# Loading q, k and v by pairs of tiles, two tokens to a partition, in a fused attention and maxout-FFN kernel on one NeuronCore

## The chip, the cores and the metric

The kernel runs on one core of one Trainium2 chip. The metric is the device time of one execution in microseconds; the number given for a kernel is the median of its runs. A core has five engines that run queues of their own and wait for each other through semaphores: PE (TensorE: matmuls, transposes), DVE (VectorE), ACT (ScalarE), POOL (GpSimd) and SP (SyncE, which here only issues DMAs). Each engine takes its instructions strictly in the order of its queue, so an instruction that waits holds all that stand behind it on that engine.

## The reference

Sliding-window attention with a few global keys, and after it a feed-forward layer that takes the maximum of three products. Four batches, 8 heads, 768 tokens, 64 elements to a head; 3072 tokens of 512 in the FFN; all f32 in DRAM.

```python
scores = scale * np.matmul(q, k.transpose(0, 1, 3, 2))
is_global = pos[None, :] < 8                     # n_global
is_local = (rel >= 0) & (rel < 96)               # n_local; rel = query - key
dist = np.where(is_global & ~is_local, 96.0, np.abs(rel))
scores = np.where(is_global | is_local, scores - slopes[h] * dist, -1e9)
a = softmax(scores)
x = (a @ v).transpose(0, 2, 1, 3).reshape(3072, 512)
h = np.maximum(np.maximum(x @ w1, x @ w2), x @ w3)      # 512 -> 768, three times
out = h @ w_out                                         # 768 -> 512
```

## The kernel before, in words

**Tiles.** The 3072 tokens are 24 tiles T of 128 (six to a batch; t is T's place in its batch). A query tile needs the keys of its own tile and of the one before (`ds` = 0 and 1 in `u_S`, L267); the 8 global keys are put into the key columns 0 to 7 of the middle tiles (`put_kg`, L208) and the same rows of v (`put_vg`, L217), where the window would leave them out. g is a group of four heads. Tiles are gathered into seven FFN chunks of 4, 2, 2, 4, 4, 4 and 4 tiles (`sizes`, L89), so an FFN product has a free width of 512, or 256 in chunks 1 and 2.

**One tile's path.** `load` (L159) fetches q and k of a tile, `load_v` (L168) v, each row of 64 f32 (256 bytes) to its own place, one token to a partition. For the first 12 tiles `load_part` (L150) fetches q and k of groups of 2 or 4 tiles (`GROUPS`, L91), with 2 or 4 tokens to a partition, and `u_x` (L225) puts the tokens into their plain order when it copies the transposes out of PSUM (the strided copy at L242). `cast` and `cast_part` make bf16 of it. q and k come to have the head's elements on the partitions either by PE transposes (`u_x` L238, `u_X` L260) and a copy out of PSUM (L242, L262, L263, L265), or by a DMA transpose (L249, from SP's queue). Then:

- S: scores of one g into one two-bank PSUM slot (L282), 16 matmuls for the two g of a tile with t > 0; ACT's exp from PSUM into `P` (L287).
- M: `P` times a mask that has the decay, the window and the global keys in it (L306, L308, DVE). The masks are made in the head from `rbase`, the distances (L452 to L471), by ACT (`u_K`, L299). Some early tiles have a bias added by a matmul instead (`u_B` L294, L274) and skip M.
- A: `P` times v with a column of ones, 16 matmuls (8 where t is 0; L321, L324), into one of the same two slots; then the reciprocal and the product that divides (L330, L331, DVE) into `xb`.
- T: `xb` transposed, by PE (L348) and a copy (L349) or by DMA (L339), into `xT`.
- F: one of 18 units of a chunk (6 column blocks f, 3 weights j), four matmuls (L360) into one PSUM bank. j = 0 is copied to SBUF by ACT (L365), j = 1 and 2 are maxima on DVE (L367, L369), the last into `ht`.
- O: six matmuls of one output tile (L375), a copy out (L381), and the output DMA. E is the last chunk's outputs: two tiles' sums are first run over five of the six rows of `ht`, then over the last.

**PSUM.** Two two-bank slots for S and A (`sp0`, `sp1`), three banks `h` for F and O, one bank `tp` for transposes: eight banks. A pool hands out its buffers in turn, and a unit issues its PE work and the operation that empties the bank together.

**The order of the work** is written out by hand: `SCHEDULE` (L25 to L57) is a list of units, each a letter and numbers, and `tc.manual_schedule()` takes them in that order, which is the order on every engine's queue. The last number of many units names the engine: 0 ACT, 1 DVE, 2 POOL, 3 and 4 special ways (for `X` and `T` 4 is the DMA transpose). So `F3.4.1` is chunk 3, block 4, weight 1, and `C14.1.2` the cast of tile 14's v on POOL.

```python
def u_F1(c, f, j):
    ...
    for dm in range(4):
        nc.tensor.matmul(ps, w123[f // 2][:, dm, j, ...], xT[c][:, dm], ...)
    if j == 0:
        nc.scalar.copy(h01, ps)
    elif j == 1:
        nc.vector.tensor_max(h01s[c, f], h01s[c, f], ps)
    else:
        nc.vector.tensor_max(ht[c][:, f], h01s[c, f], ps)
```

Of the kernel before, what the change touches and what calls it, by code (L numbers as in the profile page):

```python
# [60 lines left out]
def kernel(  # L61
# [18 lines left out]
    assert NG == 8 and NL == 96  # L80
# [21 lines left out]
    raw_pool = ctx.enter_context(tc.tile_pool(name="raw", bufs=5))
    rawv_pool = ctx.enter_context(tc.tile_pool(name="rawv", bufs=6))
    cast_pool = ctx.enter_context(tc.tile_pool(name="cast", bufs=5))
    qkT_pool = ctx.enter_context(tc.tile_pool(name="qkT", bufs=2))
    p_pool = ctx.enter_context(tc.tile_pool(name="pp", bufs=6))
    z_pool = ctx.enter_context(tc.tile_pool(name="zz", bufs=4))
    xb_pool = ctx.enter_context(tc.tile_pool(name="xb", bufs=3))
    xT_pool = ctx.enter_context(tc.tile_pool(name="xT", bufs=3))
    stage_pool = ctx.enter_context(tc.tile_pool(name="stage", bufs=3))  # L110
    ht_pool = ctx.enter_context(tc.tile_pool(name="ht", bufs=2))
    h01_pool = ctx.enter_context(tc.tile_pool(name="h01", bufs=4))
    ost_pool = ctx.enter_context(tc.tile_pool(name="ost", bufs=6))
    psS = ctx.enter_context(tc.tile_pool(name="psS", bufs=1, space=bass.MemoryType.PSUM))
    psH = ctx.enter_context(tc.tile_pool(name="psH", bufs=3, space=bass.MemoryType.PSUM))
    psT = ctx.enter_context(tc.tile_pool(name="psT", bufs=1, space=bass.MemoryType.PSUM))
# [42 lines left out]
    def load(T):  # L159
# [5 lines left out]
        for i, src in enumerate((q, k)):  # L165
            nc.sync.dma_start(out=r[:, i], in_=src[b, :, sl, :].rearrange("h s d -> s h d"))
# [344 lines left out]
```

## Time and profile before

| | |
|---|---|
| median of 3 runs | 181.25 us (181.25 to 181.27) |
| span of the profiled execution | 179.4 us |
| time of the profiled execution | not given on the page; the median stands 1.85 us above the span |
| first and last FFN matmul (L360) start | 23.5 and 170.3 us |
| busy: PE, DVE, ACT, POOL | 169.3, 121.2, 103.1, 38.0 us |
| HBM read, written | 25.17 MB, 6.29 MB |
| loads of q, k, v by tile, 256 KB each | 48, landing 4.3 to 5.1 us after issue (medians) |
| loads of q, k by part, 512 KB each | 12, landing 7.2 to 7.5 us after issue (medians) |
| DMA transposes on SP | 9 of qkT, 11 of xT; 1.2 us each to issue |

The profile is one execution. A line of a group gives the source line, the engine, the operation and its tiles with their shapes, the count, the busy time and the mean length of one, and then the idle time of that engine just before these instructions with what ended it. "PE h L360 <- DVE h L367" in a list of waits means that PE's matmul at L360 waited for DVE's operation at L367. The chain is followed back from the last instruction: each piece is the work, or the wait, that the next one could not start without. The stretch tables give the busy time of each engine between two moments, the clock that was granted to PE (1.00 is full) and the moved bytes.

### The profile page before, as it was taken

The numbers are of one execution on the slowest core, as the hardware profiler recorded it, in microseconds if no ns is written. First come the engines' busy times: TensorE is split into PE (matmuls) and PEld (weight loads), VectorE is DVE, ScalarE is ACT, GpSimd is POOL, SyncE is SP. The second block draws the span as 40 slices with busy tenths as digits, with TensorE's granted clock in tenths as the row PEclk, the third lists the DMA queues.
The fourth block names the chain that finished last, engine by engine and source line by source line (L and its number), as shares of the span: only waits on it lengthen the run. The fifth ranks groups of instructions, "written<-read, shape, count | busy, mean of one in ns | idle before, by whom it ended". The sixth has DMA issues, their size and how long they took to land.

```text
span 179.4 us, 3954 instructions
## 1 busy us (share of the span) xinstructions
PE 169.3 (94%) x1534; PEld 97.0 (54%) x1556; DVE 121.2 (68%) x240; ACT 103.1 (57%) x158; POOL 38.0 (21%) x64
## 2 busy tenths in 40 slices
PE   7788798999999999999999999999999999999992
PEld 2365653557877687844555455455444555444451
DVE  4636948987788879748879447979358886136610
ACT  4899697336897858565745836361772643440131
POOL 6254225532512011410007024100030301000000
PEclk9969999999999999999999999999999999999999
DMA  4999999999993999999644999869859884600005
GB/s 139 290 263 250 358 322 382 318 361 345 249 189 123 254 264 218 209 177 237 111 90 117 133 242 247 173 131 182 177 130 282 169 139 146 235 28 4 0 32 202
DMA packets 83586, 35.51 MB, mean 198 GB/s; under 512 B 66160, under 2 KB 78320, under 8 KB 83568
## 3 DMA queue, kind: packets, MB, share of 16 engines
q1 hardware_dynamic: 83424, 35.20, 82.9%
q8 instruction: 12, 0.20, 0.5%
q10 hardware_dynamic: 144, 0.07, 0.1%
q14 instruction: 6, 0.05, 0.1%
HBM read 25.17 MB, written 6.29 MB: 175 GB/s over the span
## 4 chain that ended last, share of the span: by engine, by line
PE 81%; SPq 5%; DVE 5%; DMA 3%; ACT 2%; issue 2%; ACTq 0%
PE h L360 49%; PE po L375 17%; PE sp L282 5%; DMA rawp<-in_k_dram 3%; SPq L157 3%; PE op L321 3%; PE op L324 2%; SPq L173 2%; DVE P L306 2%; PE tpp L238 1%; PE xtp L348 1%; DVE xb L331 1%; ACT P L287 1%; ACT h L365 1%; DVE qkT L242 1%
## 5 line engine op out<-in xcount | busy, mean ns | idle before, releaser
L360 PE MATMUL h<-xT,w 128*128 128x512 bf16 (+1 forms) x491 | 99.9, 348 | 1.3 <-DVE h L367 0.6
L360 PEld LDWEIGHTS <-w 128*128 128x128 bf16 x504 | 46.8, 98 | 41.3 <-issue 0.9
L287 ACT ACTIVATE P<-sp 128x1024 bf16<-128x1024 f32 (+1 forms) x48 | 43.3, 955 | 18.2 <-PE sp L282 17.8
L367 DVE TENSOR_TENSOR h<-h,h 128x512 bf16<-128x512 bf16 (+1 forms) x42 | 25.4, 610 | 23.7 <-PE h L360 15.8
L365 ACT CAST h<-h 128x512 bf16<-128x512 f32 (+1 forms) x42 | 21.7, 532 | 23.0 <-PE h L360 22.4
L375 PE MATMUL po<-wo,ht 128*128 128x512 bf16 (+2 forms) x147 | 33.0, 362 | 0.5
L306 DVE TENSOR_TENSOR P<-P,wmask 128x1024 bf16<-128x1024 bf16 x37 | 25.9, 730 | 6.3 <-ACT P L287 6.2
L369 DVE TENSOR_TENSOR ht<-h,h 128x512 bf16<-128x512 bf16 (+1 forms) x42 | 25.1, 607 | 4.0 <-PE h L360 3.3
L375 PEld LDWEIGHTS <-ht 128*128 128x128 bf16 x156 | 14.1, 98 | 13.9
L381 ACT COPY ost<-po 128x512 f32<-128x512 f32 (+2 forms) x19 | 10.6, 562 | 18.0 <-PE po L375 17.9
L331 DVE TENSOR_TENSOR xb<-op,rz 128x512 bf16<-128x512 f32 x24 | 16.6, 692 | 0.8
L282 PE MATMUL sp<-qkT 64*128 64x128 bf16 x352 | 15.0, 220 | 1.6 <-ACT qkT L242 1.4
L282 PEld LDWEIGHTS <-qkT 64*128 64x128 bf16 x352 | 10.2, 95 | 10.1 <-issue 8.0
L321 PEld LDWEIGHTS <-P 128*128 128x128 bf16 x192 | 12.7, 99 | 2.5 <-DVE va L188 0.4
L197 POOL CAST qkb<-raw 128x1024 bf16<-128x1024 f32 x7 | 7.2, 1036 | 28.5 <-DMA raw<-in_k_dram 28.5
L321 PE MATMUL op<-va,P 128*128 128x65 bf16 x160 | 12.5, 193 | 0.5 <-ACT P L287 0.3
L220 POOL COPY va<-vaf 8x260 int32<-8x260 int32 x13 | 6.5, 501 | 27.8 <-PE op L324 27.8
L242 ACT COPY qkT<-tpp 128x1024 bf16<-128x1024 bf16 (+1 forms) x10 | 9.5, 971 | 3.6 <-PE tpp L238 3.4
L324 PEld LDWEIGHTS <-P 128*128 128x128 bf16 x160 | 10.4, 97 | 1.7 <-issue 0.2
L324 PE MATMUL op<-va,P 128*128 128x65 bf16 x128 | 9.9, 193 | 0.0
L381 DVE COPY ost<-po 128x512 f32<-128x512 f32 (+1 forms) x7 | 4.4, 631 | 7.4 <-PE po L375 7.4
L188 POOL CAST va<-rawv 128x512 bf16<-128x512 f32 x9 | 5.5, 616 | 15.7 <-DMA rawv<-in_v_dram 15.5
(68 smaller groups left out, 116.2 us busy)
## 6 DMA issues: line engine op xcount, KB each, us to landing
rawv<-in_v_dram SPq DMA_DIRECT2D x24, 256.0 KB, 5.1
out_dram<-ost SPq DMA_DIRECT2D x23, 256.0 KB, 2.4
rawp<-in_q_dram SPq DMA_DIRECT2D x6, 512.0 KB, 7.2
rawp<-in_k_dram SPq DMA_DIRECT2D x6, 512.0 KB, 7.5
wst<-in_moe_w_dram SPq DMA_DIRECT2D x3, 1024.0 KB, 9.9
raw<-in_q_dram SPq DMA_DIRECT2D x12, 256.0 KB, 4.3
raw<-in_k_dram SPq DMA_DIRECT2D x12, 256.0 KB, 5.0
wst<-in_moe_w_dram SPq DMA_DIRECT2D x3, 512.0 KB, 8.9
```

Of the source, the lines that this page charges most:

```text
L282: nc.tensor.matmul(sp[:, hh, j2, ds], qT(T - ds, 1)[hsl, jp], qT(T, 0)[hsl, jp], start=not how, stop=True, skip_group_check=True)
L287: nc.scalar.activation(P[:, :, 0:n], sp.rearrange("p a b d n -> p (a b) d n")[:, :, 0:n], AF.Exp, bias=0.0, scale=scale)
L306: nc.vector.tensor_mul(P, P, wmask[:, g, :, 0:2])
L321: nc.tensor.matmul(o, P[:, i, 0], heads(va[T])[:, h], start=True, stop=(t == 0), skip_group_check=True)
L324: nc.tensor.matmul(o, P[:, i, 1], heads(va[T - 1])[:, h], start=False, stop=True, skip_group_check=True)
L331: nc.vector.tensor_tensor(out=x.rearrange("p (g h) d -> p g h d", g=2), in0=o4[:, :, :, 0:64], in1=rz[:, :, :, None].to_broadcast([128, 2, ...
L360: nc.tensor.matmul(ps, w123[f // 2][:, dm, j, (f % 2) * 128:(f % 2) * 128 + 128], xT[c][:, dm], start=(dm == 0), stop=(dm == 3))
L365: nc.scalar.copy(h01, ps)
L367: nc.vector.tensor_max(h01s[c, f], h01s[c, f], ps)
L369: nc.vector.tensor_max(ht[c][:, f], h01s[c, f], ps)
L375: nc.tensor.matmul(po, ht[c][:, f, tt * 128:(tt + 1) * 128], wo[:, f, cols], start=(f == 0), stop=(f == NF - 1))
L381: copy(ost, po)
```

## The change

All 24 tiles are loaded by pairs: a load `l` fetches q, k or v of two tiles (512 KB, or 256 KB for half of the heads in the first pair's q and k), with two neighbouring tokens on a partition, so that a run in DRAM is 512 bytes. Partitions 0 to 63 then hold the first tile of the pair, 64 to 127 the second. The order of the tokens inside a tile (the even ones, then the odd ones, e = 0 and 1) is kept: in q, k, v, the masks (`rbase` is made for that order), the scores, `xb` and `xT`; the FFN's last maximum writes `ht` with a step of two and so restores the plain order. v is cast by halves (one tile and one e, 64 partitions). `put_vg` becomes two copies.

The loads, casts, transposes and their copies out of PSUM, and the operations that empty the banks of S, A, F and O, are units of their own now, and each unit names the buffer it takes (`@slot`). PSUM is a ring `h` of four banks (F, O and the transposes) and two two-bank slots `sp` (S and A). The engine of h's first copy is chosen by the unit. DMA transposes are 14 of q and k (128 columns in, 16 blocks of 64 out) and 16 of `xb`. `SCHEDULE` is new as a whole.

```diff
-    def load(T):
...
-        for i, src in enumerate((q, k)):
-            nc.sync.dma_start(out=r[:, i], in_=src[b, :, sl, :].rearrange("h s d -> s h d"))
+    def u_l(slot, a, G, p):
+        h0, nh = span(p)
+        b, g = divmod(G, NT // 2)
+        r = ring("rv" if a == 2 else "r", slot, [128, 1024], FP32, "raw" + "qkv"[a])
+        r = r[:, 0:nh * 128].rearrange("i (h x) -> i h x", h=nh)
+        raw[a, G, p] = r
+        src = (q, k, v)[a][b, h0:h0 + nh, g * 256:(g + 1) * 256, :]
+        nc.sync.dma_start(out=r, in_=src.rearrange("h (i e) d -> i h (e d)", e=2))
+    def u_c(slot, a, G, p, how):
...
+        dst = qb[G][:, a, h0 // 2:(h0 + nh) // 2].rearrange("i j e (s d) -> i j e s d", s=2)
+        copies[how](dst, raw[a, G, p].rearrange("i (j s) (e d) -> i j e s d", s=2, e=2))
+    def u_v(slot, T, e, how):
+        G, t = divmod(T, 2)
+        src = raw[2, G, 2][64 * t:64 * t + 64].rearrange("i h (e d) -> i e h d", e=2)[:, e]
+        copies[how](heads(va(T))[64 * e:64 * e + 64, :, 0:D], src)
+    def u_x(slot, G, a, p):
...
+        for j in range(nh // 2):
+            for e in range(2):
+                nc.tensor.transpose(tp[:, :, j, e], qb[G][:, a, h0 // 2 + j, e], identb)
+    def u_X(slot, T):
...
+        nc.sync.dma_start_transpose(
+            out=qkT[G][:, t].rearrange("c a j (e i) -> c (a j e) i", e=2),
+            in_=qb[G][64 * t:64 * t + 64].rearrange("i a j e x -> i (a j e x)"))
+    def u_V(slot, T, how):
+        b, t = divmod(T, NT)
+        for e in range(2):
+            rows = slice(64 * e, 64 * e + NG // 2)
+            copies[how](words(va(T)[rows]), words(va(b * NT)[rows]))
+    def u_f(slot, c, f, j, how):
...
+            copies[how](h01, ps)
         elif j == 1:
             nc.vector.tensor_max(h01s[c, f], h01s[c, f], ps)
         else:
-            nc.vector.tensor_max(ht[c][:, f], h01s[c, f], ps)
+            dst = tile_ht(c, slot)[:, f].rearrange("p (t i e) -> p t e i", e=2, i=64)
+            nc.vector.tensor_max(dst, h01s[c, f].rearrange("p (t e i) -> p t e i", e=2, i=64),
+                                 ps.rearrange("p (t e i) -> p t e i", e=2, i=64))
-        pos = [psH.tile([128, DM], FP32, name="po", tag="h") for _ in range(min(2, n - 1))]
+        def bank(w):
+            h[0] += 1
+            return ring("h", (slot + h[0] - 1) % RINGS["h"], [128, w], FP32, "po")
...
+        for ds in range(2):
+            for e, P in halves:
+                nc.gpsimd.iota(rbase[P, ds], base=128 * ds - e, pattern=cols, channel_multiplier=-2,
+                               allow_small_or_imprecise_dtypes=True)
+        for e, P in halves:
+            nc.gpsimd.affine_select(rbase[P, 0], rbase[P, 0], base=-e, ...)
+            nc.gpsimd.affine_select(rbase[P, 0], rbase[P, 0], base=NL - 1 + e, ...)
+            nc.gpsimd.affine_select(rbase[P, 1], rbase[P, 1], base=NL - 129 + e, ...)
```

Three places of the new queue, as far as the prediction speaks of them. Small letters that follow a unit's capital empty its bank (`e` S, `n` A, `t` and `u` T, `f` F, `o` O, `s` the output DMA; `x` and `y` transposes and their copy); `Z` and `X` are DMA transposes.

```diff
-    D3.0 K4 K0 l1.0 B1.2 B2.1 D5.6 B7.1 K2 l1.1 K1 B0.1 D2.0 K3 v0 K5 D0.6 B3.1 B5.1 c0.0.1 D4.0 K6 c1.0.2
...
+    l1.0.0@0 l1.0.1@1 B6.2 B5.2 c1.0.1.1@0 K7 B7.2 D6.512@0 l0.0.1@2 K0 c0.0.1.2 D6.512@1 l0.0.0@3 K2
+    c0.0.0.2 K3 l2.0.2@0 B3.1 c1.0.0.1 K1 B2.1 K4 x0.1.1@2 x0.0.1@3 l0.1.2@4 l1.1.2@5 K6 x0.1.0@0 B4.1
...
-    F4.1.2 C17.1.2 O3.1.1 A17.1 F4.2.2 F4.3.2 S18.0.0 M18.0 S18.1.0 M18.1 F4.4.0 T16.4 T17.4 F4.4.1
...
+    S18.0.0@1 S18.1.0@0 e18.1@4 s0.2 s0.1 e18.0@5 F4.2.2@0 f4.5.1.1 S17.0.0@0 e17.0@0 v20.1.2 f4.1.1.1
+    v18.1.1 S17.1.0@1 e17.1@2 l1.11.2@0 F4.2.0@2 m18.1.1 V16.2 f4.1.2.1 F4.2.1@3 f4.2.0.1@3 S19.1.0@0
...
-    F6.4.1 F6.2.2 F6.3.2 F6.5.0 F6.4.2 F6.5.1 F6.5.2 E
+    f6.0.2.1 F6.5.0@3 F6.2.2@2 f6.2.1.1 s5.1 s4.3 f6.2.2.1 f6.5.0.0@1 F6.5.1@1 f6.5.1.1 f6.5.2.1 E@4
```

More of the change, by code (lines that the diff above doesn't have):

```diff
@@ L98, with ring @@
         chunks.append(list(range(first, first + n)))
-    NCH = len(chunks)
-    persist = ctx.enter_context(tc.tile_pool(name="persist", bufs=1))
[L102 to L116, printed above, removed]
+    last = len(chunks) - 1
+    pools = {}
+    for name in RINGS:
+        space = {"space": bass.MemoryType.PSUM} if name in ("sp", "h") else {}
+        pools[name] = ctx.enter_context(tc.tile_pool(name=f"p_{name}", bufs=1, **space))
+    persist = ctx.enter_context(tc.tile_pool(name="persist", bufs=1))
+    def ring(name, slot, shape, dtype, label):
+        assert 0 <= slot < RINGS[name]
+        return pools[name].tile(shape, dtype, name=label, tag=f"{name}{slot}")
     identf = persist.tile([128, 128], FP32, name="identf")
@@ L389, in u_E, with u_O, u_o @@
[L389 to L396 removed]
+    def u_O(slot, c, tt):
+        pos[c, tt] = ring("h", slot, [128, DM], FP32, "po")
+        f2_mm(pos[c, tt], c, tt, range(NF))
+    def u_o(slot, c, tt, how):
+        osts[c, tt] = ring("ost", slot, [128, DM], FP32, "ost")
+        copies[how](osts[c, tt], pos[c, tt])
```

458 lines of the change are left out of this document (210 added, 248 removed).

## The prediction, made before the changed kernel was run

> **What bounds the kernel now.** I read the busy shares first, then the chain of work that ended last, then that chain in order of time, the busy times by stretch, and last the costs of single operations. The page of the profile:
>
> ```profile
> span 179.4 us, 3954 instructions
> PE 169.3 (94%) x1534; PEld 97.0 (54%) x1556; DVE 121.2 (68%) x240; ACT 103.1 (57%) x158; POOL 38.0 (21%) x64
> ...
> PE 81%; SPq 5%; DVE 5%; DMA 3%; ACT 2%; issue 2%; ACTq 0%
> ```
>
> PE is busy 94% and the chain is 81% PE. The pieces of the chain in order of time (start, length, what) show where it is not:
>
> ```profile
> 10.26 6.25 DMA rawp<-in_k_dram
> 27.80 2.49 DVE P L306 x2
> ...
> 155.12 7.55 PE h L360 x35
> 162.72 7.93 PE h L360 x36
> 170.66 2.81 PE po L375 x13
> 173.52 2.37 PE po L375 x22
> ```
>
> Until 16.5 us the chain is loads; from the first FFN matmul (L360, at 23.47 in the timeline) it is PE without a break but for one stall of .6 us at 30 us, to the last copy, which starts at 175.95; its output DMA ends the span 3.45 us later. So there are three parts: head 23.47, body 152.5, tail 3.45. The busy times by stretch say how near the other engines are:
>
> ```profile
> 31.00:60.00 29.00, 28.79 (x307) 19.79 (x311) 23.98 (x46) 18.88 (x31) 9.66 (x12) 1.00 0.96 265
> 60.00:100.00 40.00, 39.69 (x428) 25.05 (x436) 31.25 (x65) 25.73 (x43) 7.79 (x13) 1.00 0.95 181
> 100.00:140.00 40.00, 39.58 (x306) 19.60 (x310) 26.91 (x50) 21.14 (x31) 5.26 (x7) 1.00 0.90 191
> ```
>
> After the stretch and its length the columns are PE, weight load, DVE, ACT, POOL, clock, DMA share, GB/s. PE is full; DVE is next, 24.0 of 29 us (83%) early on, 67% later. A change that takes work from PE gains it only while DVE keeps up.
>
> The span is 179.4; the runs' median is 181.25. The page gives no time for the profiled execution, so I put 1.85 us around the span, before and after alike. Differences of 0.2% (.36 us) are about what a measurement here can tell from none.
>
> **PE: what goes.** The qk transposes fall from 120 to 80 and those of xb from 52 to 32, as ten more tiles go by DMA transposes. Nearly all is behind the first FFN matmul: 108 transposes there become 48. In the chain a group of eight took .45 us, so one is .056, and 60 are **−3.3 us**. All other matmuls keep number and shape (S 352, A 352, FFN 504, O 156, by their weight loads), but for four bias matmuls of the head, which lies behind loads anyway.
>
> **DVE: what comes.** 17 copies of h to h01 move from ACT (11 of 512 at .686 as the maximum of that shape, 6 of 256 at .417: 10.0); v casts go from 3 to 18 because each now covers 64 partitions and one of two tokens (15 x .424 = 6.4; I price a half by its elements per partition, since the 8-partition memset of rbase took .17 and the 128-partition copy .15); four more output copies (4 x .688 = 2.8); masks 44 to 46 (1.2). Off go four qk casts less two halves (−1.9), two biases (−.9), three V copies (−.8) and some G, xT, qkT and rbase copies (−2.8). Sum **+14**, 121 to 135.
>
> ```profile
> L306 DVE TENSOR_TENSOR P<-P,wmask 128x1024 bf16<-128x1024 bf16 x37 | 25.9, 730 | 6.3 <-ACT P L287 6.2 <-ACT wmask L299 0.2
> L367 DVE TENSOR_TENSOR h<-h,h 128x512 bf16<-128x512 bf16 x30 | 20.4, 686 | 20.8 <-PE h L360 13.4 <-ACT P L287 7.3
> L369 DVE TENSOR_TENSOR ht<-h,h 128x512 bf16<-128x512 bf16 x30 | 20.1, 683 | 2.8 <-PE h L360 2.1
> ...
> L381 DVE COPY ost<-po 128x512 f32<-128x512 f32 x6 | 4.1, 688 | 3.2 <-PE po L375 3.2
> ...
> L242 DVE COPY qkT<-tpp 128x1024 bf16<-128x1024 bf16 x2 | 2.4, 1219 | 0.0
> ...
> L265 DVE COPY qkT<-tp 128x1024 bf16<-128x1024 bf16 x1 | 0.7, 683 | 0.0
> ```
>
> What counts is where it falls. I summed each stage's units, in queue order, with these row prices. Chunks 1 and 2 (256 wide, six maxima for .437 us of matmuls each): DVE 31.2 before, 35.8 after; PE 33.5 after, 35.1 with the small gaps that the chain shows behind scores. Operations standing back to back start every .60 to .64 us where each is booked at .69, so the 35.8 are some 32 to 33 of work against 35.1 of PE: 93%. At 83% nothing was lost; here each late release of a bank is a PE stall. Floor 0 (DVE always finds the next bank ready), ceiling 4 (every operation at its booked length plus the .2 us from a matmul's end to its reader's start): **+1.2**, nearer to the floor, because the pitch is measured. Chunk 4: DVE 24.2 against 25.4 of PE (before 20.5 and 26.5): 0 to 1.5, **+.3**. Chunks 3, 5 and 6 stay under 83%: 0.
>
> **ACT and POOL.** ACT loses some 19 us and is bound nowhere in the body. POOL goes from 38 to about 60: 19 more V copies at .50, nine more v casts at .616, two biases at 1.42, casts of the rest. It is still at a third; the cover is its idle time, and without it a late cast delays a transpose two tiles ahead. SP issues 22 loads less and ten DMA transposes more (1.24 each); it waits for nothing but free buffers, and the next output DMA stands behind a transpose that waits for its cast: cost 0 while the six output stages have room, one landing (D) if not.
>
> **Waits in the new queue.** Scores and outputs of attention share two slots of two banks each, and the queue has S18, one FFN unit, S17. S17.0 needs the slot of S18.1, whose exp takes 1.03 (row L287) plus .2 to start: 1.23 against .86 of FFN. S17.1 needs the slot of S18.0, whose exp stands behind the first on ACT: .75 more. **+1.1**, floor .4 if ACT starts on the other exp first. Two A units (A10, A14) stand 1.15 us behind scores in their slot: **+.2**, 0 to .3.
>
> At the end, E takes bank 0 first, that of the last third product of chunk 6 (F6.5.2). Its maximum is the last of the queue on DVE, behind that of F6.5.1, PE's last unit before E. So E begins .2 + .62 + .69 + .05 = **+1.6** after F6.5.1. Before, E started at 170.49 while the last maximum ran to 171.38, since only the sixth step of its sums reads that row and its banks were free. Floor .9 (only one maximum left to wait for), ceiling 1.8. Three reuses of a bank after one FFN unit in chunk 6 have .86 for .95: **+.2**.
>
> **Head.** Loads of 512-byte runs replace v's and part of q's and k's 256-byte ones. In the first half of the trace stretches of v and weight loads moved 230 to 384 GB/s, so order, not rate, decides; the first pairs land as before. But rbase now takes four iotas (.235 each) and six selects (.295), as halves of 64 partitions at the full price: ready at 5.2, not 3.64. Behind it three biases stand on POOL (1.42 each, to 9.4) and ahead of POOL's first q casts, so S0 is at 11 where it was at 9.34; the queue then has slack on ACT, and by my walk the exps of tile 3 end at 21.5 and the first FFN matmul follows POOL's V copies and weight cast at 24.0 (23.1 if a POOL bias is the .55 of a DVE one, 25.8 with all late): **+.5**. The clock there, from the busy times by stretch:
>
> ```profile
> 11.00:13.00 2.00, 1.82 (x21) 1.56 (x18) 1.35 (x3) 2.00 (x3) 1.20 (x2) 0.50 1.23 276
> ```
>
> The granted clock was .50 here, behind a thin stretch. Another gap may put such a stretch later, at up to +.8; it is inside the 25.8. [...]
>
> **Sum.** −3.3 + 1.2 + .3 + 1.1 + .2 + 1.6 + .2 + .5 = **+1.8**: span 181.2, time **183.0**.
>
> **Rivals.**
> A. *Faster: DVE keeps up, and PE's gain stays.* If the .62 pitch holds in chunks 1 and 2 and ACT's lighter load lets S17's slots come free, the sum is −3.3 + 1.6 + .2 + .5 = −1.0, and with the old .6 stall gone and the head .4 early rather than .5 late, −2.5: 178.7 to 180.2, middle **179.5**. For it: DVE had 5 us idle in 29 where it was fullest. It decides at a DVE load of about 95% in chunks 1 and 2. Against: the same row's waits for PE do not go away.
>
> B. *The last maximum slows.* L362 of the changed kernel writes ht with a step of two elements. The two PSUM copies above cost 1219 strided and 683 not. The maximum takes 683 for 512 elements, 1.33 ns each, the slow copy's 1.19: it has no fast rate to lose, so I take 0. Doubled, 30 x .54 + 12 x .28 = 19.6 more DVE, of which half is cover: about **192**. [...]
>
> C. *POOL slows DVE's masks.* M took .68 alone (18.28), .96 beside a POOL cast (11.90), two took 2.49 at 27.80 with POOL busy throughout. POOL's 22 us more, mostly beside masks, would add .28 to .56 to a dozen of them, about 3.6 of DVE, of which the two tight stages pass on 1.5: **184.5**. [...]
>
> D. *Loads or DMA transposes late.* Each transpose took SP 1.24 to issue and landed 3.2 later; ten more, and the queue's pairs land later than single tiles. One of them in the open adds 3.2 to the forecast: **186**.
>
> **How the numbers follow.** Forecast .45, A .30, C .12, B .05, D .08. From the forecast's own spread (181.2 to 184.8) .06 falls within 0.2% and .01 below, from A .02 within: faster .29, same .08, slower .63. The range leaves out B, A's lowest, and the far ends of C and D: 178.9 to 187.0.
>
> **What would show it.** First FFN matmul at 24.0 (not before 23.1); in PE's waits about 1.6 us on the last maximum before E, some 1.1 on an exp at S17, several short ones on DVE in chunks 1 and 2; DVE busy about 135; L362 at 683; M's mean at or under .75 (over .85 is C). It would be wrong if PE has no waits for DVE in chunks 1 and 2 (A), or if the waits are for loads (D).

## The result, and the profile after

The changed kernel took 189.55 us (median of 4 runs, 188.52 to 190.77) against 181.26 (181.25 to 181.48): ratio **1.0456** [1.0413, 1.0498]. The forecast was 183.0, the range 178.9 to 187.0. Of kernels 2, 5, 8 and 10 further down one execution in four was disturbed and of 12 two; the ratios leave these out, so 12's rests on two executions.

The page of the changed kernel:

```profile
span 187.4 us, 3816 instructions
PE 169.3 (90%) x1470; PEld 95.0 (51%) x1492; DVE 138.5 (74%) x266; ACT 87.1 (46%) x131; POOL 66.0 (35%) x104
...
PEclk9955579999999999999999999999999999999999
...
PE 70%; DVE 12%; POOL 5%; DMA 5%; issue 4%; ACT 2%; SPq 1%; POOLq 0%; DVEq 0%
```

PE has the same busy time in 8 us more, and its part of the chain is 70% instead of 81%. The clock row tells where: the four slices of 4.7 us from 9 to 28 us are below 9. The matmul records show the three parts of the span:

| us | before | after |
|---|---|---|
| first FFN matmul starts (end of the head) | 23.47 | 29.68 |
| from there to PE's last matmul's start | 152.2 | 154.2 |
| from there to the end of the span | 3.8 | 3.5 |

So **6.2 us are lost in the head and 2.0 in the body**. The head's chain, in order of time (start, length, what), pieces under .9 us left out:

```profile
5.77 1.54 POOL bias L283
...
7.37 1.34 POOL bias L283
...
8.95 1.06 issue
...
10.67 1.46 PE tp L205 x12
...
17.67 1.71 PE tp L205 x16
...
23.83 0.97 PE sp L251 x2
...
28.58 1.05 POOL w L426
```

The "issue" at 8.95 is POOL's third bias (the records have the three from 5.77 to 9.95). Then come POOL's first q cast and the transposes that wait for it. What PE waited for, of the whole span (total, times, longest), shows that wait and the body's three:

```profile
PE tp L205 <- POOL qb L188: 4.2, 1, 4.2
PE po L367 <- DVE ht L362: 1.6, 1, 1.6
PE h L343 <- ACT ost L381: 1.6, 1, 1.6
PE xtp L328 <- DVE xb L313: 1.2, 2, 1.0
...
PE po L367 <- DVE xT L331: 0.9, 1, 0.9
```

The busy times by stretch (columns as in the prediction) show PE thin and the clock at half:

```profile
8.00:16.00 8.00, 3.81 (x44) 2.86 (x44) 4.58 (x12) 4.92 (x9) 5.31 (x7) 0.54 1.19 292
16.00:24.00 8.00, 6.49 (x68) 4.76 (x68) 6.40 (x12) 3.77 (x5) 3.50 (x5) 0.50 1.09 356
24.00:32.00 8.00, 7.34 (x92) 4.47 (x92) 5.80 (x11) 5.81 (x8) 6.59 (x9) 0.90 1.09 355
```

PE's 3.81 us of 8 is at .54, no engine is full, and DMA is at 1.1 to 1.2 throughout. In the kernel before, the stretch from 8 to 16 us had PE busy 6.23 and the clock at .79:

```profile
8.00:16.00 8.00, 6.23 (x81) 4.45 (x79) 3.23 (x6) 7.51 (x10) 4.51 (x6) 0.79 1.25 267
```

In the body I summed the pitch from one weight load to the next by the kind of the first (1,344 loads of before and 1,284 of after):

| us in the body | FFN (504) | outputs (155) | S (280) | A (296) | transposes |
|---|---|---|---|---|---|
| before | 93.2 | 29.5 | 9.8 | 11.8 | 7.9 (108) |
| after | 96.9 | 31.3 | 10.1 | 12.2 | 3.6 (48) |

The transposes give 4.2 us, more than the 3.3 forecast. This is spent again: 3.7 in FFN pitches and 1.8 in those of the outputs, which is where PE's waits fall.

### The profile page after: what moved, and what is told of

Its sections match the earlier page's. It is cut to its first block, busy times and chain, and to the rows that moved or that the text cites. A ratio compares the mean times of both kernels' runs of the same rounds, so it can differ in the third digit from the quotient of the medians.

```text
span 187.4 us, 3816 instructions
## 1 busy us (share of the span) xinstructions
PE 169.3 (90%) x1470; PEld 95.0 (51%) x1492; DVE 138.5 (74%) x266; ACT 87.1 (46%) x131; POOL 66.0 (35%) x104
## 4 chain that ended last, share of the span: by engine, by line
PE 70%; DVE 12%; POOL 5%; DMA 5%; issue 4%; ACT 2%; SPq 1%; POOLq 0%; DVEq 0%
PE h L343 41%; PE po L367 14%; PE sp L259 5%; PE op L301 3%; PE tp L205 3%; DMA out_dram<-ost 3%; DMA rawv<-in_v_dram 2%; DVE P L275 2%; PE op L304 2%; DVE ht L362 2%; DVE xb L313 2%; POOL bias L283 2%; ACT P L266 1%; DVE vaf L193 1%; PE sp L251 1%
## 5 line engine op out<-in xcount | busy, mean ns | idle before, releaser
L362 DVE TENSOR_TENSOR ht<-h,h 128x512 bf16<-128x512 bf16 (+1 forms) x42 | 26.8, 646 | 6.2 <-PE h L343 5.6
L357 ACT CAST h<-h 128x512 bf16<-128x512 f32 (+1 forms) x25 | 13.1, 537 | 30.0 <-PE h L343 29.0
L239 POOL COPY va<-vaf 4x260 int32<-4x260 int32 x32 | 13.8, 430 | 31.2 <-PE op L304 27.4
L259 PE MATMUL sp<-qkT 64*128 64x128 bf16 x352 | 16.5, 231 | 1.5 <-ACT P L266 0.8
L193 POOL CAST va<-rawv 64x512 bf16<-64x512 f32 x20 | 14.2, 711 | 8.5 <-DMA rawv<-in_v_dram 5.2
L188 POOL CAST qb<-rawq 128x1024 bf16<-128x1024 f32 (+1 forms) x10 | 12.3, 1237 | 4.7 <-DMA rawq<-in_q_dram 4.4
L357 DVE CAST h<-h 128x512 bf16<-128x512 f32 (+1 forms) x17 | 10.1, 592 | 4.5 <-PE h L343 4.3
L301 PE MATMUL op<-va,P 128*128 128x65 bf16 x160 | 13.2, 197 | 0.1
L188 POOL CAST qb<-rawk 128x1024 bf16<-128x1024 f32 x7 | 7.6, 1079 | 14.3 <-issue 9.4
L381 ACT COPY ost<-po 128x512 f32<-128x512 f32 x10 | 5.9, 587 | 13.9 <-PE po L367 8.3
L233 POOL COPY qkT<-kg 128x32 bf16<-128x32 bf16 x7 | 2.0, 287 | 28.3 <-PE sp L259 25.3
```

Source lines behind the costliest of these rows:

```text
L188: copies[how](dst, raw[a, G, p].rearrange("i (j s) (e d) -> i j e s d", s=2, e=2))
L193: copies[how](heads(va(T))[64 * e:64 * e + 64, :, 0:D], src)
L259: nc.tensor.matmul(sp[:, hh, j2, ds], qT(T - ds, 1)[hsl, jp], qT(T, 0)[hsl, jp], start=not how, stop=True, skip_group_check=True)
L301: nc.tensor.matmul(o, P[:, i, 0], heads(va(T))[:, h], start=True, stop=(t == 0), skip_group_check=True)
L357: copies[how](h01, ps)
L362: nc.vector.tensor_max(dst, h01s[c, f].rearrange("p (t e i) -> p t e i", e=2, i=64), ps.rearrange("p (t e i) -> p t e i", e=2, i=64))
```

## The experiments

First FFN matmul and last matmul (starts) are from each run's profile. Where two kernels have the same PE queue, I compare the starts of the n-th weight load in both; a step in that difference is a stall, or a stretch at a lower clock, that only one of them has. "A10" in an expectation is the unit A of tile 10, and so on. Each kernel has one profile. Kernels with the same head had their first FFN matmul at 29.37 to 29.89 (changed, 4, 5, 8), at 26.92 to 27.33 (6, 7, 9) and at 26.57 and 27.16 (11, 12), so a difference under some .6 us in that column says nothing.

| kernel | ratio to before [95%] | first FFN | last matmul |
|---|---|---|---|
| before | 1 | 23.47 | 175.65 |
| changed | 1.0456 [1.0413, 1.0498] | 29.68 | 183.89 |
| 1 biases behind the q casts | 1.0419 [1.0402, 1.0437] | 27.68 | 183.00 |
| 2 zeros | 1.0427 [1.0407, 1.0446] | – | – |
| 3 both | 1.0444 [1.0425, 1.0462] | 28.85 | 184.00 |
| 4 other bank for E | 1.0397 [1.0366, 1.0428] | 29.89 | 183.21 |
| 5 two early output DMAs | 1.0532 [1.046, 1.0604] | 29.37 | 186.11 |
| 6 head in another order | 1.0383 [1.0332, 1.0433] | 27.16 | 182.39 |
| 7 = 4 + 5 + 6 | 1.0227 [1.0204, 1.025] | 27.33 | 179.86 |
| 8 h's first copy on ACT | 1.0597 [1.0559, 1.0635] | 29.38 | 188.31 |
| 9 = 7 + v of pair 8 early | 1.0274 [1.0232, 1.0317] | 26.92 | 180.57 |
| 10 = 9 without biases | 1.0289 [1.0272, 1.0306] | – | – |
| 11 = 10 + zeros in the head | 1.0323 [1.0299, 1.0348] | 26.57 | 182.01 |
| 12 = 11 + copy of tile 7 on ACT | 1.0204 [1.0179, 1.0229] | 27.16 | 179.54 |
| 13 before, v first | 1.0089 [1.0074, 1.0104] | 26.39 | 177.81 |
| 14 before, POOL biases | 1.0083 [1.0057, 1.0109] | 25.97 | 177.38 |
| 15 k first | 1.0305 [1.026, 1.035] | 28.29 | 181.38 |
| 16 = 15 + zeros | 1.0267 [1.0245, 1.0288] | 27.35 | 180.66 |
| 17 before, rbase by halves | 1.0062 [1.0046, 1.0079] | 25.1 | 176.5 |
| 18 before, 13 + 14 + 17 | 1.0176 [1.0161, 1.0192] | 27.86 | 179.3 |

### The POOL biases and the clock (1, 2, 3)

```diff
-    l1.0.0@0 l1.0.1@1 B6.2 B5.2 c1.0.1.1@0 K7 B7.2 D6.512@0 ...
-    c0.0.0.2 K3 l2.0.2@0 B3.1 ...
+    l1.0.0@0 l1.0.1@1 c1.0.1.1@0 K7 D6.512@0 ...
+    c0.0.0.2 B6.2 B5.2 B7.2 K3 l2.0.2@0 B3.1 ...
```

> The changed kernel with its three POOL biases (1.34 to 1.54 us each, 5.77 to 9.95) put behind POOL's two first q casts instead of ahead of them. Theory 1 (the biases start the loss: PE idles 4.2 us to 10.67, and the clock is at .50 from 8.5 to 25.5): q casts at about 7, PE's wait shrinks to 1 or 2 us, the granted clock stays at 1.00 or comes back by 14, first FFN matmul at 24 to 26 where it was 29.7, time 184 to 186 against 189.5. Rival (the head is bound by loads, by POOL's V copies and weight cast at 26 to 29.6, or by the pairs as such): the first FFN matmul moves by less than 1.5 us, time over 188.

The second has one unit more (`D16.512@1` ahead of `x0.0.1@3`), the third both edits.

> The changed kernel with 16 matmuls of zeros (128x512) in PE's queue ahead of the transposes that wait for POOL's q cast; nothing else moved, so the cast still ends at 10.63. If the clock is most of the loss: it stays at 1.00 past 10.7, the PE work from 10.7 to 25.5 (12 us busy at .50) shrinks to 6, first FFN matmul at 25 to 27, time 185 to 187. If the wait itself is most of it, or if the clock drops anyway because PE is thinly used from 13 to 20: the first FFN matmul stays past 28.5, time over 188.3.

> Both edits: biases behind the q casts and 16 matmuls of zeros ahead of the transposes. If wait and clock add: first FFN matmul at 23.5 to 25, time 183 to 184.5. If they are one cause (the wait is what drops the clock), the same as the biases alone, within .5 us, and the zeros (3.5 us at full clock) may even cost up to 1 us where the q cast comes before they end.

The casts went to 7.3, and the first FFN matmul came 2.0 us sooner; the time fell by under .4% and neither expectation held. Theory 1 was a third of the 6.2 at most. With the zeros too the clock held to 16.5 us and was at half for 3.4 us where the changed kernel has 17.1, and still the first FFN matmul was at 28.85, later than without: the zeros delayed the transposes to 9.95. So neither edit finds the larger part. In the same profile POOL's cast of pair 2's q stands in the chain:

```profile
20.68 0.61 POOL va L193
...
21.33 0.72 POOL va L193
...
22.11 3.00 POOL qb L188
...
25.15 1.08 PE tp L205 x16
```

A cast of 128x1024 that takes 1.04 us by itself took 3.00 beside DVE's work, and it stood behind a copy (L239) that waited 5.8 us for A1. By its ratio the zeros alone (2) changed nothing measurable.

### E's bank (4)

```diff
-    ... f6.5.0.0@1 F6.5.1@1 f6.5.1.1 f6.5.2.1 E@4
+    ... f6.5.0.0@1 F6.5.1@1 f6.5.1.1 f6.5.2.1 E@6
```

> The changed kernel with E's first bank moved from 0 (that of F6.5.2, emptied by the last maximum on DVE) to 2 (F6.2.2, emptied long before). Theory (PE's wait of 1.56 us ahead of E is for the bank alone): the wait goes, since two sums over five rows of ht (2.2 us) cover the last maximum; span 1.5 us shorter, time 188.0 against 189.5. Rival (E waits for the last row of ht anyway, or the next banks make it wait later): no more than .5 us.

By the weight loads E came 1.67 us sooner relative to the last FFN matmul, and its wait is gone from PE's list. Of it .7 shows in this span: the head was .2 later here, and the waits near 100 us .8 longer. The next experiments look at that place.

### The head's order, the output stage, DVE's copies (5 to 8)

```diff
 5
-    ... e13.0@1 l1.7.2@5 ...      s0.0 v16.1.1 s1.1 F4.1.0@1 ...
+    ... e13.0@1 s0.0 s1.1 l1.7.2@5 ...      v16.1.1 F4.1.0@1 ...
 6
-    x0.0.0@1 B1.1 K5 y0.1.1.1@0 y0.1.0.1 G0.1 v1.1.2 y0.0.1.0 S0.1.0@0 ...
-    ... A0@0 ... c0.1.2.2@1 w1.1@1 m1.1.1 n0@0 t0@2 x1.0.2@3 l2.2.2@2 c1.1.2.1 x1.1.2@0
-    u0.0@0 m1.0.1 A1@1 V1.2 v3.0.2 y1.1.2.1@1 n1@1 v3.1.2 c0.2.2.2@2 ...
+    x0.0.0@1 B1.1 K5 y0.1.1.1@0 y0.1.0.1 G0.1 v1.1.2 v1.0.2 c0.1.2.2@1 B6.2 B5.2 B7.2 y0.0.1.0 S0.1.0@0
+    ... x1.0.2@3 A0@0 ... c1.1.2.1 y1.0.2.0@1 m1.1.1 n0@0 x1.1.2@0 t0@2 l2.2.2@2
+    u0.0@0 m1.0.1 y1.1.2.1 B0.1 S2.1.0@0 e2.1@4 A1@1 c0.2.2.2@2 V1.2 v3.0.2 n1@1 ...
 8 (17 times)
-    f0.4.0.1@2
+    f0.4.0.0@2
```

> The changed kernel with two output DMAs (tile 0 of chunk 0 and tile 1 of chunk 1) issued on SP at about 75 us, where their sums have been copied out, and not at about 103 behind four DMA transposes and two v loads. Theory (PE's 1.6 us at 107, matmul of chunk 4 behind ACT's output copy, is a missing output stage: the copy waits for the landing, 4.8 us, of an output DMA that SP issued late): PE's wait on the output copy goes, 1.1 to 1.7 us less, about 188.0 against 189.5. Rival (the DMA queue as such is late there, and v's or the transposes' landings stop PE next): under .5 us.

> The changed kernel with the same units in the head in another order: POOL casts q and v of the first pairs ahead of its three biases, and q of pair 2 ahead of the copy of the global rows of v that waits for A1; DVE casts v and multiplies the first masks ahead of a bias; PE transposes pair 1 ahead of T0; the scores of tile 2 come ahead of A1. Theory 2 (the head's loss is in the order: units that wait stand ahead of units that could go): first FFN matmul at 24 to 26 (29.7 in the changed kernel, 27.7 with the biases alone moved), span 2 to 4 us shorter, time 186 to 187.5, as part of it is lost again at the late output DMA at 103. Rival (POOL's and DVE's work in the head has grown too large for any order: 19 us of POOL before the first FFN matmul): first FFN matmul at 27 or later, time over 188.3.

> The new order of the head, the two early output DMAs and the other bank for E together. If the three losses are separate (head 3.5 to 5.5, output stage 1.1 to 1.7, E 1.6): 182 to 184. If a further bound stands behind them (DVE in chunks 1 and 2, v loads): over 185.

> The changed kernel with its 17 copies of h's first product on DVE given back to ACT (as before the change): DVE 10 us less, ACT 9 us more. If DVE is what the body waits for in chunks 1, 2 and 4, as the prediction has it: .5 to 1.5 us shorter, about 188.5. If DVE's load costs nothing there: no change or up to 1 us longer, as the copies stand behind exps of 1.03 us on ACT.

**5**: the wait for the output copy went, and another of 2.2 us came 5 us ahead of it. What PE waited for from 30 us on:

```profile
PE po L367 <- DVE ht L362: 2.2, 1, 2.2
PE po L367 <- DVE xT L331: 0.9, 1, 0.9
PE sp L259 <- DVE xb L313: 0.2, 1, 0.2
```

and the chain ahead of it in the same kernel:

```profile
98.28 0.56 SPq L334
...
98.87 4.96 DMA rawv<-in_v_dram
...
103.86 0.42 DVE va L193
...
104.31 0.74 DVE ht L362
...
105.09 2.01 PE po L367 x6
```

SP issues v of pair 8 at 98.87, behind DMA transposes (L334); it lands 4.96 us later; DVE's cast of it stands in DVE's queue ahead of chunk 3's last maximum, and PE's outputs of chunk 3 wait for that. The theory (a missing stage) was true of the one wait and wrong about the time. The six matmuls at 105.09 take 2.01 where six take 1.3 at full clock (.216 each): behind this wait the granted clock was at half for 3.4 us. The clock rows of 5, 8 and 11 show such a stretch in the body, each behind a wait of 1.8 to 2.4 us (from 105.9 us in 5, 106.6 in 8, 93.3 in 11):

```profile
PEclk9955899999999999999999699999999999999999
```

```profile
PEclk9755799999999999999999699999999999999999
```

```profile
PEclk9999969999999999999969999999999999999999
```

The changed kernel, whose waits there are 1.6 us at most, has none behind 26 us.

**6**: the first FFN matmul at 27.16, the time 188.35, 1.2 us less. Theory 2 expected 24 to 26 and 186 to 187.5; these are, by a hair, the numbers of its rival (27 or later, over 188.3), that the work of POOL and DVE is too large for any order. **7** brings PE's last matmul 4.0 us sooner than in the changed kernel (179.86 for 183.89): 2.4 of it in the head, the rest in the body. Its time of 185.47 misses the 182 to 184 expected of it.

**8** fell the other way: ratio 1.0597, though DVE was busy 9 us less (129.4). By the weight loads it loses .5 at 50, .6 at 54 and .8 at 60 us, where copies now stand behind exps, and 3.1 at 103, at the load of v, about half of this by the half clock. The wait of .9 for tile 7's copy stays. So chunks 1 and 2 wait as before with less work on DVE, and the copies are better there.

### SP's queue, biases, zeros, tile 7 (9 to 12)

```diff
 9
-    ... f3.1.1.1 X14@3 ...      Z13@1 l2.8.2@2 m15.0.1 ...
+    ... f3.1.1.1 l2.8.2@2 X14@3 ...      Z13@1 m15.0.1 ...
10 (and all eight B units go)
-    S3.0.1@0 e3.0@0 S3.1.1@1 e3.1@2 v2.0.1 m2.1.1 m2.0.1 ...
+    S3.0.0@0 e3.0@0 S3.1.0@1 e3.1@2 v2.0.1 m2.1.1 m2.0.1 m3.0.1 m3.1.1 ...
11 (six more like it)
-    S0.1.0@0
+    D5.512@2 S0.1.0@0
12
-    u7.1@2
+    u7.0@2
```

> The kernel with the new order of the head, the two early output DMAs and the other bank for E, and now also v's load of pair 8 issued on SP two DMA transposes and one wait earlier (ahead of the DMA transposes of tiles 14, 15 and 16 and not behind them). Theory 3 (the body's loss at 100 us is SP's queue: the load is issued at 97 to 100 because it stands behind transposes that wait for casts; DVE then waits for v with the last maximum of chunk 3 behind it, and PE's output sums for that maximum, 1.6 to 2.2 us): PE's wait at 100 us goes, 183.5 to 184.2 against 185.5. Rival (the DMA engines are full there, so v lands no earlier): within .5 us of 185.5.

> The kernel before it in this list, with no biases at all: the scores of tile 3 are multiplied by the mask as those of the other tiles are (two more masks on DVE, .68 each), and the eight biases (three on POOL 4.4 us, five on DVE 1.9 us) and four bias matmuls go. If POOL's and DVE's load holds the head: first FFN matmul .5 to 1.5 us sooner than 27.3, time 182.5 to 183.5. If the head is a chain of waits (exp, mask, A, division, transpose) with idle engines beside it: within .4 us.

> As without biases, and 24 matmuls of zeros (128x512) in PE's gaps from 8 to 19 us, so that the granted clock holds: it was .50 from 10 to 23 us in the kernel with the new order, where PE was busy 15 of 20 us. Theory 2b (with the waits gone, the halved clock sets the rest of the head: 6 us of work at .50 that would take 3): clock 1.00 through 20 us, first FFN matmul at 24 to 25.5, time 180.5 to 182. Rival (PE's work at half speed is hidden behind ACT, DVE and POOL): under .5 us of gain, or a loss as the zeros delay transposes.

> As the kernel before it in this list, and the copy of tile 7's transposed x out of PSUM on ACT and not on DVE: PE waited .9 us for it at 64 us (output sums of chunk 0 need its bank). If that wait is DVE's load there (the prediction's step on chunks 1 and 2): .5 to .9 us shorter. If ACT is as late (exps of 1.03 ahead of it): no change.

**9** was not faster than 7. Against 7 its PE lost 1.67 us at 90 and won 1.14 at 103. What PE waited for from 28 us on, in 7 and then in 9:

```profile
PE po L367 <- DVE ht L362: 1.6, 1, 1.6
PE po L367 <- DVE xT L331: 0.9, 1, 0.9
```

```profile
PE sp L259 <- DMA qkT<-qb: 1.4, 1, 1.4
PE po L367 <- DVE xT L331: 0.9, 1, 0.9
PE h L343 <- DVE ht L362: 0.5, 1, 0.5
PE sp L259 <- DVE xb L313: 0.3, 1, 0.3
```

The wait for v became one for the DMA transpose of tile 14, which now lands behind v's 512 KB. This is the rival: from 84 to 105 us the DMA engines are full (their share there is 1.07 in the changed kernel), and here putting one transfer first made another late. **10** and **11** gained nothing (10 by its ratio alone). 11 lost 2.1 us more than 9 at the same DMA transpose, though its wait is 1.8 for 1.4: most of the rest is the stretch at half clock behind it. **12** took the wait for tile 7's copy away (.9 in 7 and 9, gone here), as expected; the rest of its difference to 11 is the landing at 90 us (a wait of 1.1 for 1.8) and that clock.

### Parts of the head by themselves (13 to 18)

```diff
13 (in the kernel before)
-    D3.0 K4 K0 l1.0 B1.2 ... K3 v0 K5 ... x0.1.0 v1 l2.1
+    D3.0 K4 K0 v0 v1 l1.0 B1.2 ... K3 K5 ... x0.1.0 l2.1
14 (in the kernel before)
-    B2.1 D5.6 B7.1 K2 ... B3.1 B5.1 c0.0.1 D4.0
+    B2.1 D5.6 B7.2 K2 ... B3.1 B5.2 c0.0.2 D4.0
15 (head of 10, without v's early load of 9, with 12's copy; loads and PE order)
-    c0.0.0.2 K3 l2.0.2@0 c1.0.0.1 ... l0.1.2@4 l1.1.2@5 ...
+    c0.0.0.2 K3 l0.1.2@4 c1.0.0.1 ... l1.1.2@5 l2.0.2@0 ...
17 (in the kernel before)
-        nc.gpsimd.iota(rbase[:, 0, :].bitcast(mybir.dt.int32), base=0, ...)
+        for ds in range(2):
+            for p0, P in halves:
+                nc.gpsimd.iota(rbase[P, ds, :].bitcast(mybir.dt.int32), base=128 * ds - p0, ...)
```

> The kernel before, with v of tiles 0 and 1 (2 loads of 256 KB) issued on SP ahead of the loads of q and k of tiles 2 and 3, as the changed kernel's order has it (v of pair 0 ahead of q and k of pair 1). Theory 4 (part of the head's loss is k of the second pair landing later: 10.5 us before, 12.5 in the changed kernel with the new order, where DVE's cast of it heads the chain): k lands at 12 to 12.7, first FFN matmul 1 to 2 us later than 23.5, 182.3 to 183.3 against 181.3. Rival (the order of loads is hidden by casts): under .4 us.

> The kernel before, with three biases on POOL instead of one and the first q cast on POOL behind them, as the changed kernel has it. POOL's biases then run from 3.8 to 8.1, the cast ends at about 9.1 (6.3 before), PE idles 2.5 us, and the granted clock may fall from then on. If that is what a bias ahead of the first cast costs: first FFN matmul 1.5 to 3 us later, 182.8 to 184.3. If the head has slack there: under .5 us.

> The changed kernel with another bank for E, the two early output DMAs, tile 7's transpose copied by ACT, no biases, and a head in the order of the kernel before: q and k of pair 1 loaded and cast ahead of v of pair 0, the scores of tile 2 ahead of both A units. Theory 4: k of pair 1 lands at 10.5 instead of 12.5, first FFN matmul at 25 to 26 (27.2 with v first), 183 to 184. Rival (DVE's work in the head, nearly without a gap from 12 to 24 us, sets it): 26.8 or later, 184.5 to 186.

> As the kernel before it in this list, with 16 matmuls of zeros in PE's gaps between 8 and 20 us. If the clock, and not DVE, is the rest: granted clock 1.00 to 23.5, first FFN matmul .7 to 2 us sooner than without them. If DVE sets the head: no change, or up to .5 us longer.

> The kernel before, with the distances rbase made by halves of 64 partitions: four iotas and six selects where there were two and three, the same values. In the changed kernel rbase was ready at 5.6 us where it was 3.64. If POOL's price goes by the instruction, rbase is ready 1.3 to 1.5 us later. If the masks' exps on ACT, which stand ahead of ACT's first copy of qkT, then head the chain: first FFN matmul 1 to 1.5 us later, 182.0 to 182.8. If they have slack: within .4 us.

> The kernel before, with three steps of the changed head at once: rbase by halves, v of the first two tiles ahead of q and k of the next two, and three biases on POOL ahead of the first q cast. By themselves the second moved the first FFN matmul by 2.9 us and the third by 2.5 (23.47 to 26.39 and 25.97). If they add: 28 to 29.5, as in the changed kernel (29.68), time 184.5 to 186. If they hide each other: 26.5 to 27.5, 183 to 184, and the rest of the changed head is in its own order and its halves of v.

These are the runs that settle a part of it. **13**: POOL's casts of the second pair began at 11.06 and 12.87 where they began at 8.68 and 10.54, and the first FFN matmul came 2.9 us later. **14**: the first cast ended at 9.1, PE waited 2.6 us for it, the clock was at .50 from 12 to 16 us, and the first FFN matmul came 2.5 us later. **17**: rbase was ready 1.4 us later, and the first FFN matmul 1.65 later. **18**, all three: +4.4 us, less than their sum of 7.1 and between the two outcomes expected, so the waits hide each other in part. In 13, 14, 17 and 18 the half clock also lasted longer (6.8 to 10.2 us, 3.4 in the kernel before); that share is not taken apart. The chain of 18 in the head, pieces in order:

```profile
5.17 1.50 POOL bias L294
...
6.73 1.41 POOL bias L294
...
8.20 1.17 POOL bias L294
9.37 1.00 POOL qkp L182
...
10.41 1.05 PE tpp L238 x8
...
11.48 1.94 ACT qkT L242 x2
```

The same three biases, then the cast, then the transposes, as in the changed kernel. Each of 13, 14, 17 and 18 gave back .77 us at 30 us, where the kernel before waits .6 for a maximum on DVE: a late head finds that bank free. So 18 ends 3.6 later and not 4.4.

**15 and 16** tell clock from engines. From 8 to 28 us, first 15, then 16:

```profile
8.00:16.00 8.00, 4.29 (x56) 3.38 (x57) 5.46 (x11) 6.38 (x11) 2.37 (x3) 0.67 1.20 291
16.00:24.00 8.00, 5.31 (x72) 4.42 (x71) 6.28 (x12) 3.84 (x5) 3.74 (x6) 0.50 1.09 359
24.00:28.00 4.00, 4.00 (x51) 3.08 (x48) 3.08 (x8) 1.97 (x4) 2.48 (x5) 0.52 1.10 354
```

```profile
8.00:16.00 8.00, 5.50 (x71) 3.18 (x72) 5.27 (x11) 5.96 (x11) 3.72 (x4) 1.00 1.13 291
16.00:24.00 8.00, 4.78 (x80) 3.17 (x78) 7.21 (x15) 4.75 (x6) 4.31 (x6) 1.00 1.10 354
24.00:28.00 4.00, 3.30 (x51) 2.19 (x52) 3.22 (x7) 1.91 (x4) 3.07 (x6) 1.00 1.08 360
```

A clock of 1.00 all along against .50 from 11 us on goes with a first FFN matmul .94 us earlier (28.29 to 27.35), less what the zeros delay; it is one profile of each, and the ranges of the two ratios overlap. At full clock all along the FFN still starts 3.9 us later than in the kernel before, so the clock is not the main part. DVE is then busy 7.2 of 8 us from 16 to 24. In 15 the clock stayed at .50 from 16 to 24 us with PE busy 5.31 of 8; what brings it back is not shown. That q and k of the second pair come first in 15 did not help, though they landed at 8.67 and 10.48 (10.65 and 12.46 in 12): v of the first pair now landed at 12.29 (8.66 in 12), and DVE's two casts of it (12.44 to 14.07) stand in DVE's queue ahead of the copy of qkT that the scores of tile 2 wait for. The time is above what either side expected.

## Why the prediction was wrong

**Head: +.5 forecast, ceiling 2.3, +6.2 measured. This is the step that failed.** The prediction had the parts right: rbase at 5.2 (5.6), biases to 9.4 (9.95), S0 at 11 (12.1). It then wrote that the queue has slack behind that, and let 1.7 us of late S0 cost .5. Runs 14 and 17 show what the delay costs: in the kernel before 2.7 us of late cast cost 2.5 of first FFN, and 1.4 of late rbase cost 1.65. The head is a chain of waits (cast, transpose, copy, S, exp, mask, A, division, transpose), and these two delays went through it nearly whole. The other failing sentence is that "the first pairs land as before": q and k of pair 1 landed at 8.63 and 10.49 before and at 10.67 and 12.47 in the changed kernel, behind v. In the kernel before, 13 shows that this costs 2.9 by itself. In the changed kernel its share is not shown: q and k of pair 1 are cast there at 12.6 and 16.9, so they waited for no load, and 15, which undoes it in a later variant, won nothing. Three steps together give 4.4 of 6.2, in the kernel before (18). The other 1.8 was not taken apart, and in the changed kernel itself no edit tried won back more than 3.1 (11). That POOL's and DVE's work is too large for any order, the rival in 6 and 15, is not ruled out by their numbers; against it speaks 10, where all eight biases went and nothing was gained. Late casts beside DVE (3.00 for 1.04) and the order of pair 1's units are where I would look.

**Clock**: named as up to .8, found at about .9 (15 to 16, one profile of each). The size was right as far as this shows; it was the smaller part.

**PE's transposes**: −3.3 forecast, −4.2 measured; the price of .056 holds as the median pitch of a transpose in both kernels. What the sum left out is the first of each group, whose pitch is longer (up to .22).

**E's bank**: +1.6 forecast, 1.6 in PE's list, 1.67 won by its removal (4). Mechanism and size hold.

**DVE in chunks 1, 2 and 4**: DVE's busy time was forecast at 135 and is 138.5. PE's waits for it in chunks 1 and 2 are .9 (tile 7's copy, 12) and two of .1, which by the pitch of the weight loads cost 1.4 where 1.2 was forecast; chunk 4 has none where .3 was. So the size was near and the mechanism narrower than I put it: single operations that came late, not a general lack, and 8 shows that less DVE work made it no faster.

**S17, A10, A14 and chunk 6's banks**: +1.5 forecast; behind 30 us PE's list has no wait for an exp. The step failed.

**DMA (rival D, .08)**: its sentence on the output DMA behind a waiting transpose was what happened at 107 us: 1.6 of PE. But the cost that I took for it was 0. It is the body's other loss, 1.6 to 2.4 us by the lists, 3.1 with the half clock behind it (8), and it did not go away by moving one transfer (5, 9).

**Rival B**: L362 took 727 where L369 took 683, not double. **Rival C**: M's mean is 730 in both, but both are mixtures: a mask alone takes .67 to .69, and beside POOL's work 20 of 38 have a mean of .77 in the changed kernel, 9 of 37 one of .86 before: some 1.6 us in all, in both. Single ones were hit hard (1.52 at 63.04 beside a POOL cast), and POOL's casts too (3.00 for 1.04 in 3). So C is there for both engines, and for the masks it did not grow.

```profile
L275 DVE TENSOR_TENSOR P<-P,wmask 128x1024 bf16<-128x1024 bf16 x38 | 27.3, 730 | 1.8 <-ACT P L266 1.8
L362 DVE TENSOR_TENSOR ht<-h,h 128x512 bf16<-128x512 bf16 x30 | 21.5, 727 | 4.0 <-PE h L343 3.6
```

Body: +1.3 forecast, +2.0 measured. Five stalls (at 65, 71, 85, 109 and 179 us; 4.3 us in PE's list) cost 5.1 by the pitch of the weight loads, where the kernel before lost .8 so: 4.3 more, about what the transposes gave. The other 1.9 is in pitches too small for the list and was not settled. No variant of the changed kernel beat the one before; the nearest, 7 and 12, are 2% slower.

## What to carry to other kernels

A change that takes work from the engine that bounds the body can be lost before the body begins: walk the head link by link, and price a late first link at its full delay until a run shows slack. Ahead of the first use, put casts ahead of set-up work on the same engine (in 14 a cast 2.7 us later cost 2.5), and load first what the next link needs; here, with v's 512 KB put ahead of them, q and k of pair 1 landed 2.0 us later (10.67 and 12.47 for 8.63 and 10.49). Where the DMA engines were full (a share of 1.07), an earlier transfer was paid by a later one (9); taking a transfer away instead of moving it was not tried here. And look at the granted clock behind a stall: in 5, 8 and 11 a wait of about 2 us in a full stretch was followed by 3.4 us at half clock.

## What the runs showed that I had not expected

- POOL's cast of 128x1024 took 3.00 us at 22 us beside two masks, a cast and a v cast on DVE, and 1.04 at 12.95 in the same kernel (3). DVE's masks pay as well: in the changed kernel one of 128x512 took .76 at 13.13, inside a POOL cast that kept its 1.04, where it takes .42 alone. In both cases the operation that began second was the long one (the 3.00 of POOL behind a v cast of .41 that DVE had begun .13 earlier); at 63.04 in the changed kernel both were, the mask with 1.52 and the POOL cast, begun at 62.48, with 1.53. So either engine paid.
- A cast of half a v tile on POOL (64 partitions) took .61 in 17 of 20 cases, like one of a whole tile before (.616): half the partitions saved nothing.
- The stretches at half clock in the heads of these profiles lasted 3.4 (the kernel before, 3, 11, 12), 6.8 (1, 14, 17), 10.2 (5, 13, 18), 13.7 (6, 7, 8) or 17.1 us (the changed kernel, 15), multiples of the 3.41 of the kernel before.
- A DMA engine took a mean of .031 us for a packet of 512 bytes, and .021 for one of 256 in the loads of the kernel before, so the pairs' loads use a quarter less engine time per byte. The ten more DMA transposes (22,528 packets of 256 bytes of a mean of .026, 14,848 before) took most of it back: the engines are busy 150.3 us on average before and 149.5 after.
- One and the same kernel scattered by 2.3 us (188.5 to 190.8) where the one before stays within .3 beside it (within .8 over all its runs). Whether the landings of the body's full DMA stretch or the stretches at half clock differ from run to run is not shown, as there is one profile of each kernel.
